# Batched attention and a gated FFN on one core: exponentials between FFN groups, two chunk orders, and a first batch loaded in four-row pieces

## The chip, the cores and the metric

One NeuronCore of a Trainium2 chip runs the whole kernel as one program. The metric is the time of an execution on the device in microseconds (us). Engines: PE (matmuls), DVE, ACT and POOL (elementwise work), SP (it only issues DMAs here); each takes its instructions in program order. ACT and POOL have queues of their own from which they can issue DMAs as well.

## The reference

Attention for 8 batches of 8 heads, 576 queries of 64 elements, with 16 "beacon" keys that every query sees and a causal mask on the other 576 keys; then a gated FFN over all 4608 tokens. Everything comes in and goes out as float32.

```python
k_all = concatenate([beacon_k, k], axis=2)          # 16 + 576 keys
v_all = concatenate([beacon_v, v], axis=2)
scores = scale * q @ k_all.T                        # per batch and head
scores = where(causal, -1e9, scores)                # causal only over the 576
a = exp(scores - scores.max(-1)); a /= a.sum(-1) + 1e-9
x = (a @ v_all), heads side by side                 # 4608 x 512
out = (maximum(x @ w_gate, 0) * (x @ w_val)) @ w_out  # 512 -> 1536 -> 512
```

## The kernel before, in words

Attention works on a pair of heads at a time: four pairs `p` per batch, head `a` of the pair on partitions 64a to 64a+63. Keys lie on partitions in the scores, so no maximum is taken: exponentials are computed directly, and the sum over keys comes from a second matmul against ones. Queries are cut into three chunks (CHUNKS): 240, 256 and 80 columns. The scores of a pair are made in four steps (STEPS): step 0 holds the whole first chunk (368 columns a head), steps 1 and 2 the middle chunk (512 and 384 columns), step 3 the last chunk against all five key tiles (400 columns). So a batch has 16 steps.

- `qk` (L257) issues a step's score matmuls into a PSUM tile `s` (two buffers). `softmax` (L267) is one exponential on ACT over both heads (L270) into `e` (four buffers) and one or two masks by affine_select on POOL (L273).
- `av` (L279) multiplies `e` with `v` and with ones into `o` (two buffers). After the last step of a chunk DVE takes the reciprocal of the sums (L300), multiplies (L302) and writes `xT`, the FFN's input; SP stores the reciprocals in `rsum` (L304) for a check at the end. `r` has three buffers.
- `Ffn.up` (L313) is one group: four gate matmuls (L320), a ReLU on ACT (L323), four up matmuls (L326), and DVE's product into `hT` (L328). Gate and up both take a buffer of the PSUM pool `f`, which has two. `Ffn.down` (L330) is a group of 12 matmuls (L333) for 128 tokens, copied by ACT (L336) and stored by SP. A tile of 512 tokens has 12 up groups and 4 down groups; the first tile is cut at token 240.
- `Batch` holds `qT`, `kT` and `v` of a batch (two buffers of each). A unit is q, k or v in a tile of 128 rows; 15 units per batch. `load` (L214, DMA at L220) fetches 128 rows of all 8 heads, 256 bytes a row and head, into `raw` (eight buffers); k and v have the 16 beacon rows in front. `cast` (L231, L238) turns it to bf16 (batch 0: k on DVE, q on ACT, v on POOL; later batches: POOL). `turn` (L240, L243) is a DMA transpose of q or k, issued by SP.
- The weights come by POOL's DMA queue (L248), cast on the way, gate and value matrix in four parts each, the output matrix `wo` whole.

The order is written out by hand (`manual_schedule`). L370 to L379 load six units of batch 0, cast and turn them, ask for the first two weight parts, and load the rest. `later` holds actions for a step: casts, turns, weights, and the `fetch` of the next batch (from step 16b+1, for batch 1 from step 3: loads at 3/4 of a step each, the cast two steps on, the turn three). The main loop (L418) goes in strides of two steps: for each of them its actions, `qk` and `softmax`; then two FFN groups from `queue`; then `av` of the two steps of the stride before. `ready` (L410) tells after which step how many tokens are through, and with that a tile's groups enter the queue. What is left of the queue runs after the loop, with a count over `rsum` after its fourth group.

Of the kernel before, what the change touches and what calls it, by code (L numbers as in the profile page):

```python
# [10 lines left out]
FP32 = mybir.dt.float32  # L11
BF16 = mybir.dt.bfloat16
# [20 lines left out]
CHUNKS = ((0, 240, 0, 0), (240, 256, 1, 2), (496, 80, 3, 3))  # L33
# [113 lines left out]
def kernel(  # L147
# [12 lines left out]
    nc = tc.nc  # L160
    B, H, S, D = q.shape
    Nb = beacon_k.shape[2]
    P = 128
    d_model = H * D
# [3 lines left out]
    NP = H // 2  # L168
    NKT = 5
    Stot = Nb + S  # L170
# [6 lines left out]
    ident = const.tile([P, P], BF16, name="ident")  # L177
# [10 lines left out]
    main = ctx.enter_context(ExitStack())  # L188
    kvq = main.enter_context(tc.tile_pool(name="kvq", bufs=2))
    stage = main.enter_context(tc.tile_pool(name="stage", bufs=8))  # L190
    half = main.enter_context(tc.tile_pool(name="half", bufs=6))
# [6 lines left out]
    f_ps = main.enter_context(tc.tile_pool(name="f_ps", bufs=2, space=bass.MemoryType.PSUM))  # L198
# [46 lines left out]
    UNITS = [(x, t) for t in range(NKT) for x in "kqv"]  # L245
# [11 lines left out]
    def qk(pr, i):  # L257
        s = s_ps.tile([P, 2, 512], FP32, name="s")
        for (kt, q0, n, c, _, _) in STEPS[i]:
            for a in range(2):  # L260
                rows = slice(a * D, (a + 1) * D)
                nc.tensor.matmul(s[:, a, c:c + n],  # L262
                                 pr.batch.kT[rows, pr.p, kt * P:(kt + 1) * P],
                                 pr.batch.qT[rows, pr.p, q0:q0 + n], start=True, stop=True)
        pr.s[i] = s

    def softmax(pr, i):  # L267
        n = STEP_COLS[i]
        e = psb.tile([P, 2, 512], BF16, name="e")
        nc.scalar.activation(e[:, :, :n], pr.s[i][:, :, :n], AF.Exp, scale=scale)  # L270
        for (kt, q0, _, c, m, base) in STEPS[i]:
            if m:
                nc.gpsimd.affine_select(  # L273
                    out=e[:, :, c:c + m], in_=e[:, :, c:c + m],
                    pattern=[[0, 2], [1, m]], compare_op=ALU.is_ge, fill=0.0,
                    base=base, channel_multiplier=-1)
        pr.e[i] = e

    def av(pr, i):  # L279
        ci = CHUNK_OF_STEP[i]  # L280
        cq0, cn, first, last = CHUNKS[ci]
        if i == first:
            pr.o[ci] = o_ps.tile([P, 2, 256], FP32, name="o")
        o = pr.o[ci]
        e = pr.e[i]
        for j, (kt, q0, n, c, _, _) in enumerate(STEPS[i]):
            kr = min(P, Stot - kt * P)
            for part in range(2):
                for a in range(2):
                    rows = slice(a * D, (a + 1) * D)  # L290
                    c0 = (2 * pr.p + a) * D
                    w = pr.batch.v[:kr, kt, c0:c0 + D] if part == 0 else ones[:kr, :]
                    nc.tensor.matmul(  # L293
                        o[rows, part, q0 - cq0:q0 - cq0 + n], w, e[:kr, a, c:c + n],
                        start=(i == first and j == 0 and part == 0),
                        stop=(i == last and j == len(STEPS[i]) - 1),
                        skip_group_check=True)
        if i == last:
            r = nrm.tile([P, 256], FP32, name="r")
            nc.vector.reciprocal(r[:, :cn], o[:, 1, :cn])  # L300
            t0 = pr.batch.b * S + cq0
            nc.vector.tensor_mul(xT[:, pr.p, t0:t0 + cn], o[:, 0, :cn], r[:, :cn])  # L302
            g = 2 * (pr.batch.b * NP + pr.p)
            nc.sync.dma_start(rsum[g:g + 2, cq0:cq0 + cn],  # L304
                              r.rearrange("(a x) n -> a x n", a=2)[:, 0, :cn])
# [38 lines left out]
    def count_in_range():  # L344

        rows = 2 * B * NP
        ge = const.tile([rows, S], FP32, name="ge")
        nc.vector.tensor_scalar(out=ge, in0=rsum, scalar1=1e-10, scalar2=None, op0=ALU.is_ge)
        nc.vector.scalar_tensor_tensor(out=ge, in0=rsum, scalar=1e10, in1=ge,
                                       op0=ALU.is_le, op1=ALU.mult)  # L350
        ok = const.tile([rows, 1], BF16, name="ok")
        nc.vector.tensor_reduce(ok, ge, op=ALU.min, axis=AX.X)
        cnt_ps = o_ps.tile([1, 1], FP32, name="o")
        nc.tensor.matmul(cnt_ps, ok, ones[:rows, :1], start=True, stop=True)
        cnt = const.tile([1, 1], mybir.dt.int32, name="cnt")
        nc.vector.tensor_copy(cnt, cnt_ps)
        return nc.values_load(cnt, min_val=0, max_val=rows,
                              skip_runtime_bounds_check_because="a count of rows")
# [6 lines left out]
    weights.append(lambda: load_w(wo, moe_w_out, 0, d_model))  # L365

    with tc.manual_schedule():
        batches = [Batch(0)]
        copies = {"k": nc.vector.tensor_copy, "q": nc.scalar.copy, "v": nc.gpsimd.tensor_copy}
        for u in UNITS[:6]:  # L370
            batches[0].load(*u)
        for u in UNITS[:6]:
            batches[0].cast(*u, copies[u[0]])
            if u[0] != "v":
                batches[0].turn(*u)
        for w in weights[:2]:
            w()
        for u in UNITS[6:]:
            batches[0].load(*u)  # L379


        later = {}

        def at(step, action):
            later.setdefault(step, []).append(action)

        for j, u in enumerate(UNITS[6:]):
            at(j // 3, lambda u=u: batches[0].cast(*u, copies[u[0]]))
            if u[0] != "v":
                at(j // 3, lambda u=u: batches[0].turn(*u))  # L390
        for j, w in enumerate(weights[2:]):
            at(j, w)

        def fetch(b, s0):
            at(s0, lambda: batches.append(Batch(b)))
            for j, u in enumerate(UNITS):
                s = s0 + j * 3 // 4
                at(s, lambda u=u: batches[b].load(*u))
                at(s + 2, lambda u=u: batches[b].cast(*u, nc.gpsimd.tensor_copy))
                if u[0] != "v":  # L400
                    at(s + 3, lambda u=u: batches[b].turn(*u))

        work, ready = [], {}
        for b in range(B):
            for c, (_, _, first, last) in enumerate(CHUNKS):
                for p in range(NP):
                    for i in range(first, last + 1):
                        work.append((b, p, i))
                done = (b * S + CHUNKS[c][0] + CHUNKS[c][1])
                ready[len(work)] = done  # L410
            if b + 1 < B:
                fetch(b + 1, 16 * b + (1 if b else 3))


        spans = [(0, 240), (240, 512)] + [(m, m + M_TILE) for m in range(M_TILE, n_tokens, M_TILE)]
        queue, have, pairs = [], 0, {}
        STRIDE = 2
        for s0 in range(0, len(work) + STRIDE, STRIDE):  # L418
            have = ready.get(s0 - STRIDE, have)
            while spans and spans[0][1] <= have:  # L420
                t0, t1 = spans.pop(0)
                f = ffn_tiles[t0 // M_TILE]
                c0, c1 = t0 - f.m0, t1 - f.m0
                queue += f.groups(c0, c1, c0 // P, c1 // P)
            for s in range(s0, s0 + STRIDE):
                for act in later.pop(s, []):
                    act()
                if s < len(work):
                    b, p, i = work[s]
                    pr = pairs.setdefault((b, p), Pair(batches[b], p))  # L430
                    qk(pr, i)
                    softmax(pr, i)
            for g in queue[:STRIDE]:
                g()
            del queue[:STRIDE]
            for s in range(s0 - STRIDE, s0):
                if 0 <= s < len(work):
                    b, p, i = work[s]
                    av(pairs[b, p], i)
        for t0, _ in spans:  # L440
            queue += ffn_tiles[t0 // M_TILE].groups(0, M_TILE, 0, M_TILE // P)
        for j, g in enumerate(queue):
            if j == 4:
                in_range = count_in_range()
            g()
# [33 lines left out]
```

## Time and profile before

| | us |
|---|---|
| Median of 2 runs | 486.41 (485.93 to 486.9) |
| Profiled execution | 484.15 |
| Its span, first to last instruction | 482.4 |
| PE busy | 394.4 (82%) |
| DVE busy | 239.8 (50%) |
| ACT busy | 190.3 (39%) |
| POOL busy | 132.0 (27%) |
| Mean granted clock of the PE, of full speed | 0.975 |

A profile has a page (busy time, 40 slices of the span, DMA queues, the chain of work that ended last) and views of the trace: timelines of an engine, windows with the busy time of each engine, waits. An idle time in brackets names what ended it. A line that begins with a time is an instruction or several alike: start and length in us, engine, line of the kernel, operation, out<-in. Several matmuls overlap in their pipeline, so the end of a group lies some 0.16 us after the PE can begin the next.

### The profile page before, as it was taken

The page shows a single profiled execution, that of the slowest core. Times are in us where ns is not written, and L with a number is a line of the kernel's source. Part 1 is how long each engine was busy: PE and PEld are TensorE (multiplying, and loading weights), DVE is VectorE, ACT ScalarE, POOL GpSimd, SP SyncE. Part 2 cuts the span into 40 slices and gives each one's busy share as a digit, 9 for nine tenths or more (in the row PEclk, how much of TensorE's full clock was granted, in tenths as well). Part 3 has the DMA queues.
Part 4 walks back from the last instruction along what each step waited for, and adds up shares of the span by engine and source line. Part 5 has one row for each costly group of instructions (what it writes and reads, how often), then busy time and mean ns, then how long its engine had stood idle before and what let it go on. Part 6 is the DMA issues. An engine that isn't in the chain of part 4 may idle for free.

```text
span 482.4 us, 9099 instructions
## 1 busy us (share of the span) xinstructions
PE 394.4 (82%) x3505; PEld 204.2 (42%) x3505; DVE 239.8 (50%) x322; ACT 190.3 (39%) x290; POOL 132.0 (27%) x293
## 2 busy tenths in 40 slices
PE   0113848777989998999899989998998899799994
PEld 0012635454434544454454445544454454244442
DVE  0033525855486448636762777277528653330320
ACT  2122414444445344534443445354444442122321
POOL 2162135343424332423251335134421110000000
PEclk9998859999999999999999999999999999899998
DMA  9999997695569257824793396439720001002002
GB/s 163 191 198 194 134 198 118 136 202 105 135 108 180 72 133 139 170 72 111 164 145 108 86 175 130 118 81 192 102 89 3 1 18 73 0 1 87 1 13 80
DMA packets 166145, 53.37 MB, mean 111 GB/s; under 512 B 155728, under 2 KB 161488, under 8 KB 166096
## 3 DMA queue, kind: packets, MB, share of 16 engines
q1 hardware_dynamic: 160320, 48.01, 49.2%
q0 software_dynamic: 5776, 4.72, 7.0%
q8 instruction: 29, 0.48, 0.4%
q14 instruction: 20, 0.16, 0.1%
HBM read 38.27 MB, written 9.44 MB: 99 GB/s over the span
## 4 chain that ended last, share of the span: by engine, by line
PE 52%; DMA 13%; SPq 9%; issue 8%; ACT 8%; DVE 5%; POOL 3%; ACTq 0%; DVEq 0%; POOLq 0%
PE f L333 19%; PE f L320 11%; PE f L326 11%; PE o L293 7%; DMA raw<-in_v_dram 6%; ACT g L323 5%; SPq L220 5%; DMA raw<-in_k_dram 5%; SPq L243 4%; DVE r L300 4%; PE s L262 3%; ACT e L270 3%; DMA raw<-in_q_dram 2%; POOL e L273 1%; POOL v L238 1%
## 5 line engine op out<-in xcount | busy, mean ns | idle before, releaser
L300 DVE RECIPROCAL r<-o 128x240 f32<-128x240 f32 (+2 forms) x96 | 129.9, 1353 | 91.4 <-PE o L293 76.3
L270 ACT ACTIVATE e<-s 128x736 bf16<-128x736 f32 (+3 forms) x128 | 103.7, 861 | 104.9 <-PE s L262 103.6
L320 PE MATMUL f<-xT,wg 128*128 128x512 bf16 (+2 forms) x480 | 116.2, 364 | 25.8 <-ACT g L323 16.4
L328 DVE TENSOR_TENSOR hT<-g,f 128x512 bf16<-128x512 f32 (+2 forms) x120 | 75.9, 633 | 106.5 <-PE f L326 92.4
L326 PE MATMUL f<-xT,wv 128*128 128x512 bf16 (+2 forms) x480 | 115.4, 364 | 9.3 <-ACT g L323 9.2
L323 ACT ACTIVATE g<-f 128x512 f32<-128x512 f32 (+2 forms) x120 | 66.8, 557 | 89.8 <-PE f L320 89.8
L333 PE MATMUL f<-wo,hT 128*128 128x512 bf16 x432 | 96.2, 379 | 0.7 <-ACT g L323 0.7
L273 POOL TENSOR_SCALAR_AFFINE_SELECT e<-e 128x256 bf16<-128x256 bf16 (+2 forms) x160 | 58.8, 388 | 96.8 <-ACT e L270 96.5
L326 PEld LDWEIGHTS <-wv 128*128 128x128 bf16 x480 | 47.6, 99 | 70.1 <-issue 26.9
L320 PEld LDWEIGHTS <-wg 128*128 128x128 bf16 x480 | 43.4, 99 | 72.0 <-issue 38.0
L238 POOL CAST half<-raw 128x512 bf16<-128x512 f32 (+1 forms) x70 | 42.4, 613 | 103.8 <-DMA raw<-in_q_dram 71.6
L293 PE MATMUL o<-e,v 128*64 128x80 bf16 (+3 forms) x704 | 57.8, 238 | 9.9 <-POOL e L273 9.8
L262 PE MATMUL s<-qT,kT 64*128 64x80 bf16 (+2 forms) x704 | 36.1, 236 | 33.3 <-DMA qT<-half 25.2
L333 PEld LDWEIGHTS <-hT 128*128 128x128 bf16 x432 | 41.1, 98 | 49.9 <-issue 2.0
L293 PE MATMUL o<-e,ones 128*64 128x80 bf16 (+3 forms) x704 | 53.9, 233 | 0.0
L293 PEld LDWEIGHTS <-v 128*64 128x64 bf16 (+1 forms) x704 | 35.6, 111 | 36.1 <-issue 35.2
L336 ACT COPY ob<-f 128x512 f32<-128x512 f32 x36 | 21.1, 586 | 67.4 <-PE f L333 67.4
L238 POOL CAST v<-raw 128x512 bf16<-128x512 f32 (+1 forms) x40 | 24.5, 613 | 61.9 <-DMA raw<-in_v_dram 61.9
L262 PEld LDWEIGHTS <-kT 64*128 64x128 bf16 x704 | 21.6, 98 | 40.1 <-issue 25.8
L302 DVE TENSOR_TENSOR xT<-o,r 128x240 bf16<-128x240 f32 (+2 forms) x96 | 34.3, 357 | 3.3
L293 PEld LDWEIGHTS <-ones 128*64 128x64 bf16 (+1 forms) x704 | 34.9, 112 | 0.1
L238 DVE CAST half<-raw 128x512 bf16<-128x512 f32 (+1 forms) x5 | 2.4, 477 | 24.5 <-DMA raw<-in_k_dram 24.5
(19 smaller groups left out, 17.0 us busy)
## 6 DMA issues: line engine op xcount, KB each, us to landing
out_dram<-ob SPq DMA_DIRECT2D x36, 256.0 KB
raw<-in_q_dram SPq DMA_DIRECT2D x32, 256.0 KB
raw<-in_k_dram SPq DMA_DIRECT2D x24, 256.0 KB
raw<-in_v_dram SPq DMA_DIRECT2D x24, 256.0 KB
raw<-in_k_dram SPq DMA_DIRECT2D x8, 224.0 KB
raw<-in_v_dram SPq DMA_DIRECT2D x8, 224.0 KB
wg<-in_moe_w_gate_dram POOLq DMA_DIRECT2D x4, 384.0 KB, 6.2
wv<-in_moe_w_val_dram POOLq DMA_DIRECT2D x4, 384.0 KB, 7.3
```

Of the source, the lines that this page charges most:

```text
L238: copy(dst, self.raw[x, t][:n])
L262: nc.tensor.matmul(s[:, a, c:c + n], pr.batch.kT[rows, pr.p, kt * P:(kt + 1) * P], pr.batch.qT[rows, pr.p, q0:q0 + n], start=True, stop=True)
L270: nc.scalar.activation(e[:, :, :n], pr.s[i][:, :, :n], AF.Exp, scale=scale)
L273: nc.gpsimd.affine_select(out=e[:, :, c:c + m], in_=e[:, :, c:c + m], pattern=[[0, 2], [1, m]], compare_op=ALU.is_ge, fill=0.0, base=base, ...
L293: nc.tensor.matmul(o[rows, part, q0 - cq0:q0 - cq0 + n], w, e[:kr, a, c:c + n], start=(i == first and j == 0 and part == 0), stop=(i == la ...
L300: nc.vector.reciprocal(r[:, :cn], o[:, 1, :cn])
L302: nc.vector.tensor_mul(xT[:, pr.p, t0:t0 + cn], o[:, 0, :cn], r[:, :cn])
L320: nc.tensor.matmul(g[:, :n], wg[:, ki, nf * P:(nf + 1) * P], x[:, ki], start=(ki == 0), stop=(ki == KM - 1))
L323: nc.scalar.activation(gs[:, :n], g[:, :n], AF.Relu)
L326: nc.tensor.matmul(u[:, :n], wv[:, ki, nf * P:(nf + 1) * P], x[:, ki], start=(ki == 0), stop=(ki == KM - 1))
L328: nc.vector.tensor_mul(self.h[:, nf, c0:c1], gs[:, :n], u[:, :n])
L333: nc.tensor.matmul(o, self.h[:, nf, ms * P:(ms + 1) * P], wo[:, nf, :], start=(nf == 0), stop=(nf == NF - 1))
```

## The change

Three things change in the order that the kernel writes out; what is computed stays.

1. In the loop, all actions and both `qk` of a stride come first; then the first `softmax`, one FFN group, the second `softmax`, the other group.
2. From batch 1 on, a batch's steps run as steps 1 and 2 of all four pairs, then steps 0 and 3 of all four pairs. Its tokens count as ready only when the whole batch is through. Batch 0 keeps its order.
3. Batch 0's q and k: rows 0 to 511 of a pair of heads are loaded with four rows to a partition (1 KB in one piece), SP's queue for k and ACT's for q; a cast regroups them, four PE transposes into an `f` tile turn them, and a copy spreads the columns (`turn_pair`). The last 64 rows, with the beacons for k, are a tile of all heads (`turn_tail`). v is loaded as before. The DMA transposes of batch 0 go. The weights' later parts are asked for two per step.

```diff
     with tc.manual_schedule():
-        batches = [Batch(0)]
-        copies = {"k": nc.vector.tensor_copy, "q": nc.scalar.copy, "v": nc.gpsimd.tensor_copy}
-        for u in UNITS[:6]:
-            batches[0].load(*u)
-        for u in UNITS[:6]:
-            batches[0].cast(*u, copies[u[0]])
-            if u[0] != "v":
-                batches[0].turn(*u)
+        b0 = Batch(0)
+        batches = [b0]
+        WIDE = 4 * P
+        rest = S - WIDE
+        start = main.enter_context(tc.tile_pool(name="start", bufs=1))
+        tails = {}
+        wide = {}
+
+        def load_pair(x, src, p, eng):
+            t = wide[x, p] = start.tile([P, 2, 4 * D], FP32, name=f"wide_{x}{p}")
+            eng.dma_start(t, src[0, 2 * p:2 * p + 2, :WIDE].rearrange("h (p r) d -> p h (r d)", r=4))
+
+        def load_tail(x, src, beacon, eng):
+            t = tails[x] = start.tile([P, d_model], FP32, name=f"tail_{x}")
+            for p0, a in ((0, src[0, :, WIDE:]), (rest, beacon)):
+                if a is not None:
+                    eng.dma_start(t[p0:p0 + a.shape[1]].rearrange("p (h d) -> p h d", d=D),
+                                  a.rearrange("h p d -> p h d"))
+
+        def turn_pair(x, p, copy):
+            h = half.tile([P, 4, P], BF16, name="half")
+            copy(h.rearrange("x r (h d) -> x h r d", d=D),
+                 wide[x, p].rearrange("x h (r d) -> x h r d", d=D))
+            ps = f_ps.tile([P, 4, P], BF16, name="f")
+            for r in range(4):
+                nc.tensor.transpose(ps[:, r], h[:, r], ident)
+            dst, off = (b0.kT, Nb) if x == "k" else (b0.qT, 0)
+            copy(dst[:, p, off:off + WIDE].rearrange("x (p r) -> x p r", r=4),
+                 ps.rearrange("x r p -> x p r"))
+
+        def turn_tail(x, copy):
+            n = rest + (Nb if x == "k" else 0)
+            h = half.tile([P, d_model], BF16, name="half")
+            copy(h[:n], tails[x][:n])
+            ps = f_ps.tile([P, NP, P], BF16, name="f")
+            for p in range(NP):
+                nc.tensor.transpose(ps[:, p, :n], h[:n, p * P:(p + 1) * P], ident[:n, :n])
+            if x == "k":
+                copy(b0.kT[:, :, Nb + WIDE:Stot], ps[:, :, :rest])
+                copy(b0.kT[:, :, :Nb], ps[:, :, rest:n])
+            else:
+                copy(b0.qT[:, :, WIDE:], ps[:, :, :rest])
+
+        load_pair("k", k, 0, nc.sync)
+        load_pair("q", q, 0, nc.scalar)
+        load_tail("k", k, beacon_k[0], nc.sync)
+        load_pair("q", q, 1, nc.scalar)
+        load_pair("k", k, 1, nc.sync)
+        for p in (2, 3):
+            load_pair("q", q, p, nc.scalar)
+        load_tail("q", q, None, nc.scalar)
+        for t in range(2):
+            b0.load("v", t)
+        for p in (2, 3):
+            load_pair("k", k, p, nc.sync)
+        for t in range(2, NKT):
+            b0.load("v", t)
+        turn_pair("k", 0, nc.vector.tensor_copy)
+        turn_pair("q", 0, nc.scalar.copy)
+        turn_tail("k", nc.vector.tensor_copy)
+        turn_pair("k", 1, nc.vector.tensor_copy)
+        turn_pair("q", 1, nc.scalar.copy)
+        b0.cast("v", 0, nc.gpsimd.tensor_copy)
+        b0.cast("v", 1, nc.gpsimd.tensor_copy)
         for w in weights[:2]:
             w()
-        for u in UNITS[6:]:
-            batches[0].load(*u)
...
-        for j, u in enumerate(UNITS[6:]):
-            at(j // 3, lambda u=u: batches[0].cast(*u, copies[u[0]]))
-            if u[0] != "v":
-                at(j // 3, lambda u=u: batches[0].turn(*u))
+        for p in (2, 3):
+            at(p - 1, lambda p=p: turn_pair("k", p, nc.vector.tensor_copy))
+            at(p - 1, lambda p=p: turn_pair("q", p, nc.scalar.copy))
+        at(3, lambda: turn_tail("q", nc.vector.tensor_copy))
+        for t in range(2, NKT):
+            at(t - 1, lambda t=t: b0.cast("v", t, nc.gpsimd.tensor_copy))
         for j, w in enumerate(weights[2:]):
-            at(j, w)
+            at(j // 2, w)
...
         for b in range(B):
-            for c, (_, _, first, last) in enumerate(CHUNKS):
-                for p in range(NP):
-                    for i in range(first, last + 1):
-                        work.append((b, p, i))
-                done = (b * S + CHUNKS[c][0] + CHUNKS[c][1])
-                ready[len(work)] = done
+            if b == 0:
+                for c, (c0, cn, first, last) in enumerate(CHUNKS):
+                    work += [(b, p, i) for p in range(NP) for i in range(first, last + 1)]
+                    ready[len(work)] = b * S + c0 + cn
+            else:
+                work += [(b, p, i) for p in range(NP) for i in (1, 2)]
+                work += [(b, p, i) for p in range(NP) for i in (0, 3)]
+                ready[len(work)] = (b + 1) * S
...
-            for s in range(s0, s0 + STRIDE):
+            now = [s for s in range(s0, s0 + STRIDE) if s < len(work)]
+            for s in now:
                 for act in later.pop(s, []):
                     act()
-                if s < len(work):
-                    b, p, i = work[s]
-                    pr = pairs.setdefault((b, p), Pair(batches[b], p))
-                    qk(pr, i)
-                    softmax(pr, i)
-            for g in queue[:STRIDE]:
-                g()
-            del queue[:STRIDE]
+                b, p, i = work[s]
+                qk(pairs.setdefault((b, p), Pair(batches[b], p)), i)
+            for j in range(STRIDE):
+                if j < len(now):
+                    b, p, i = work[now[j]]
+                    softmax(pairs[b, p], i)
+                if queue:
+                    queue.pop(0)()
```

## Rows read from the trace of the kernel before

**Rows 1.** The page: PE and DMA busy in 40 slices, tenths

```profile
PE   0113848777989998999899989998998899799994
...
DMA  9999997695569257824793396439720001002002
```

**Rows 2.** The chain of waits: start, length; down groups that open a batch's steps

```profile
119.76 5.29 PE f L333 x24
...
399.45 5.29 PE f L333 x24
```

**Rows 3.** Windows, sum over nine stretches of batch 5, 259.81 to 306.50

```profile
sum 46.69, PE 43.69 PEld 22.05 DVE 28.18 ACT 21.82 POOL 16.28; mean PE 4.85 PEld 2.45 DVE 3.13 ACT 2.42 POOL 1.81
```

**Rows 4.** Timeline of PE in batch 5

```profile
273.67 1.02 PE L320 MATMUL f<-xT,wg 128*128 128x512 bf16 x4 [0.39 <-ACT g L323]
275.37 1.02 PE L326 MATMUL f<-xT,wv 128*128 128x512 bf16 x4 [0.69 <-ACT g L323]
...
283.40 0.56 PE L262 MATMUL s<-qT,kT 64*128 64x256 bf16 x8
283.88 1.04 PE L320 MATMUL f<-xT,wg 128*128 128x512 bf16 x4
284.76 1.03 PE L326 MATMUL f<-xT,wv 128*128 128x512 bf16 x4
286.10 1.02 PE L320 MATMUL f<-xT,wg 128*128 128x512 bf16 x4 [0.31 <-ACT g L323]
```

**Rows 5.** Timeline of ACT, the stride from 283.40

```profile
283.83 1.73 ACT L270 ACTIVATE e<-s 128x1024 bf16<-128x1024 f32 x2 [2.33 <-PE s L262]
285.44 0.60 ACT L323 ACTIVATE g<-f 128x512 f32<-128x512 f32 x1
```

**Rows 6.** Timeline of DVE in batch 5

```profile
259.07 0.66 DVE L300 RECIPROCAL r<-o 128x80 f32<-128x80 f32 x1 [4.01 <-PE o L293]
...
259.92 0.65 DVE L300 RECIPROCAL r<-o 128x80 f32<-128x80 f32 x1
...
270.91 1.65 DVE L300 RECIPROCAL r<-o 128x240 f32<-128x240 f32 x1
...
272.92 1.65 DVE L300 RECIPROCAL r<-o 128x240 f32<-128x240 f32 x1
...
283.51 1.76 DVE L300 RECIPROCAL r<-o 128x256 f32<-128x256 f32 x1
285.30 0.42 DVE L302 TENSOR_TENSOR xT<-o,r 128x256 bf16<-128x256 f32 x1
286.08 0.69 DVE L328 TENSOR_TENSOR hT<-g,f 128x512 bf16<-128x512 f32 x1 [0.36 <-ACT g L323]
```

**Rows 7.** Timeline of the start, batch 0 to batch 1's first scores

```profile
11.38 1.22 SPq L243 DMA_TRANSPOSE qT<-half  x1
...
16.96 0.80 PE L262 MATMUL s<-qT,kT 64*128 64x240 bf16 x8 [16.96 <-DMA qT<-half]
...
48.35 0.36 PE L320 MATMUL f<-xT,wg 128*128 128x240 bf16 x1 [6.94 <-DVE xT L302]
...
78.09 0.49 PE L262 MATMUL s<-qT,kT 64*128 64x240 bf16 x8
```

**Rows 8.** DMA queues: packets, MB, share of 16 engines' span (q0 carries the weights)

```profile
q1 hardware_dynamic: 160320, 48.01, 49.2%
q0 software_dynamic: 5776, 4.72, 7.0%
```

**Rows 9.** Timeline of SP's queue: loads of batch 1, a turn in batch 5

```profile
58.78 3.77 SPq L220 DMA_DIRECT2D raw<-in_k_dram  x1
...
78.09 0.58 SPq L220 DMA_DIRECT2D raw<-in_v_dram  x1
...
294.53 1.24 SPq L243 DMA_TRANSPOSE qT<-half  x1
```

**Rows 10.** Timeline of POOL: a cast of batch 1

```profile
63.92 0.61 POOL L238 CAST half<-raw 128x512 bf16<-128x512 f32 x1 [13.45 <-DMA raw<-in_q_dram]
```

## The prediction, made before the result was known

> **What bounds the kernel now.** I read the page's slices first, then the chain of waits, then one batch closely, then the start. The slices [rows 1] show three stretches: about eight slices (100 us) in which the PE fills slowly while the DMA engines are full, a long plateau at 9 to 10 tenths, and a PE-bound end. In the chain [rows 2] the down matmuls that open a batch's steps return every 46.6 us from batch 2 (119.8) to the end of batch 7 (399.5): six equal periods, so one period decides 280 us. The windows over the period from 259.81 add up to 46.69 us with the PE busy 43.69 [rows 3]: 3.0 us per batch in which the PE stands still. What it waits for stands behind its rows in the timeline: the gate and the up matmuls wait for ACT's ReLU [rows 4].
>
> The timelines of PE, ACT and DVE show how. In a stride the PE does two scores steps, then gate 0, up 0, gate 1, up 1, then the output steps of the stride before. There are only two `f` buffers, so gate 1 needs ReLU 0 done. ACT has both exponentials ahead of ReLU 0: at 283.83 they start, together 1.73 us, and ReLU 0 begins at 285.44 [rows 5]; gate 1 starts at 286.10 although up 0, begun at 284.76, frees the PE some 0.87 later, at 285.63 [rows 4]. The shown idle (0.31) counts from the modelled end of the last matmul; the time lost is 0.47. Where DVE still works off two 240-column chunks (two reciprocals of 1.65 and their products [rows 6]), up 1 waits as well: 0.39 + 0.69 shown, about 1.4 lost with 0.16 on each. A batch has two such strides (2.8), two of the 0.47 kind (0.94), and about 0.3 in each of the two others (0.6): 4.3 us per batch, and 42.4 us would be left without any wait.
>
> The start: the first scores are at 16.96, the first finished FFN gate at 48.35, and batch 1's scores at 78.09 [rows 7]. From there batch 1's steps last some 41 us, to just before 119.76 [rows 2], and there the PE is not the limit: loading, casting and turning the next batch is.
>
> **Part 1: ACT's order.** PE's order stays. ACT now has exp 0, ReLU 0, exp 1, ReLU 1. Let T be the start of a stride's scores (283.40). Gate 0 starts at T+0.49, its last result is out at T+1.53; exp 0 started at T+0.43 and takes about 0.92 of the 1.73, so ReLU 0 runs T+1.57 to 2.17, and the PE, free at T+2.23, finds gate 1's buffer ready. Those waits go. ReLU 1 now stands behind exp 1, at T+3.3 to 3.9; its readers, the product 1 and a later stride, come later than that. What is late next is DVE's product 0, which frees the buffer for up 1 (PE ready at T+3.09). After a stride with a middle chunk, DVE does one reciprocal of 1.76 and a product of 0.42 and is free by T+2.32; up 0's result comes at T+2.5, so product 0 (0.69) ends at T+3.19: 0.14 lost with the signalling.
>
> **Part 2: chunks in turn.** From batch 1 on, four strides do the middle chunk, then four do the 240- and the 80-column chunk. DVE's debt per stride is then 2.2 (middle) or 2.01 + 0.85 = 2.86 (240 and 80, from the starts of successive reciprocals [rows 6]), instead of 4.0, 2.2 and 1.7. With 2.86, product 0 ends at T+3.53 and up 1 loses 0.48. Of the six strides with gate and up groups, four follow a middle chunk (4 x 0.14), one a 240/80 pair (0.48). The other one, the second of a batch, has a new wait: an FFN tile is now released only when its whole batch is through, with no group left over in the queue, and its first gate needs the 240 columns of the last pair, whose output step ended just before. That reciprocal and product are ready at about T+1.85; the gate's fourth matmul wants them at T+1.14: 0.71, and 0.14 later in the stride. Sum: 0.56 + 0.48 + 0.85 = 1.9 per batch against 4.3, so 2.4 saved; six periods give 14. Ends: all waits gone, 6 x 4.3 = 26; or up 1 waits for ReLU 1 (first rival), minus 7. The queue of groups doesn't run dry: two per stride, 16 per tile, eight strides per batch. After the last stride tile 7 meets the same late chunk without scores in front: +1.
>
> The earlier casts of the second step (all actions now come ahead of both softmaxes) can hold POOL's masks back. The masked tiles are read a stride later, 5 us on, and that covers it; the cost without this cover is the cast's wait, 1 to 5 us once.
>
> **Part 3: the first batch.** Ten DMA transposes go (SP's queue loses 10 x 1.2 us of issuing [rows 7], and the waits for casts that stand in front of them), and q and k come in four-row pieces. The queue rows [rows 8] give 0.492 x 482.4 x 16 / 160320 = 23.7 ns for a packet of the load queue (300 B on average) and 93.5 ns for one of the weights' (817 B written). The 256-byte rows of all loads are some 113,000 of those packets, the outputs 4,600; the remaining 42,000 belong to 80 transposes, 0.78 us of all engines each. Batch 0 cost 14,080 packets (20.9 us) + 7.8. Afterwards: v 4,736 and the tails 1,152 packets (8.7 us), and 2,048 packets of 1 KB, whose price the trace doesn't show: between 23.7 and 93.5 ns, 3 to 12 us; I take 7, near the middle: a piece of 1 KB is larger than either average, but the weights' packets are read at twice their size and cast. So 15.7 instead of 28.7: 13 us of DMA work less (8 to 17). "DMA: Bandwidth & Descriptors" of the Trainium skill (Specifications) says that transfers of 512 B or more run at line rate, about 27 GiB/s per engine; by that the 1 KB pieces would take 35 ns, 4.5 us in all, and the start would gain 2.5 more. No run here shows it.
>
> Forty PE transposes and some twenty copies come in. Eight scores matmuls took 0.80 at 16.96, so 0.1 each: 4 us of a PE that otherwise waits; the copies on DVE and ACT are of the size of an `hT` product or a ReLU, 0.6 to 0.7, beside the loads. "TensorE: Matmul & The Clock Gate" (Part 4: PE-mode transpose) of the Trainium skill speaks against this part: about 275 ns for one in a kernel, 11 us in all; 20 stand ahead of the first scores, which would then come 3.5 later. No transpose on the PE is in this trace.
>
> The first scores come near 10 instead of 17, the first gate near 30 to 38 instead of 48 (pair 2's load stands on PE, ACT and DVE ahead of the second scores; v tile 2's cast ahead of weights and masks on POOL). How much of that lasts to batch 1 is set by DMA: the weights (0.07 x 482.4 = 34 us of all engines) still have to come, now asked for by step 3 instead of 6, and take the share of the loads behind them. Once they are in, batch 1's units follow at the pace of SP's chain of turn, load, cast: 19.3 us for the eight from 58.78 to 78.09 [rows 9], 2.4 each. If the weights end about 11 us sooner (13 of work at a DMA share near 1.2), but one or two units fewer are in by then, 8 us remain. Bounds 0 and 16. Batch 1's own 41 us stay, being set by the same chain.
>
> **Sum.** 484.15 (the profiled execution, span 482.4) - 8 - 14 + 1 = 463. The median of the runs is 486.4, 2.3 above it; I forecast 465 for the measurement. It can tell about 2%, 9.7 us, from no change.
>
> **Rivals.** A: the wait moves to up 1. Which of the two `f` buffers up 1 gets is fixed when the program is built; at 275.37 it waited for ReLU 1 [rows 4], elsewhere for the product. ReLU 1 now ends at T+3.9: 0.86 lost instead of 0.14 in five strides, +3.6 per batch, and part 1 and 2 together cost 1.2 per batch: 465 + 22 = 487. For it: the built order did choose ReLU 1 once; against: there it was the earlier of the two, here it is later by 0.4 to 0.7. B: the start gives nothing, because weights in front of batch 0's last tiles hold POOL: 473. For it: a cast of batch 1 on POOL waited 13.5 us behind `wo` [rows 10]; against: the bytes do go. C: the start keeps all its lead (16): 457. D, the other side: the first step of a batch is now a middle chunk and needs k and q tiles 0 to 3 turned, not two of each. The turn of the fourth q tile is issued at 294.53 [rows 9], over at 295.8; a turn issued till 12.6 was used at 16.96 [rows 7], 4.4 later; so it lands near 300.2, and the next batch starts at 306.0, half a microsecond before its down group at 306.50 (the end of the window of [rows 3]): 5.8 us to spare, 3.4 when batches are 2.4 shorter. If loading slips beyond that, each us costs 7 (seven boundaries); from 3 us on the kernel is no faster than before, and at 5 us it takes 500.
>
> **How the numbers follow.** Forecast 0.55 (459 to 471), B 0.20, C 0.15, A 0.07, D 0.03. B's slow end (0.03) and A are within 2%; D alone is slower. Faster 0.87, same 0.10, slower 0.03. 453 to 477 holds the forecast, most of B and C.
>
> **What would show it.** Right: a period of about 44.3 between down groups; no wait of gate 1 for ReLU 0; up 1 waiting for DVE by 0.1 to 0.5; the fourth matmul of a tile's first gate waiting for `xT`, 0.7, once per batch; batch 1's scores near 70; scores of a batch never waiting for `qT`. Wrong: a period of 46 or more, up 1 behind ReLU 1, waits for `qT<-half` at batch starts, or batch 1 not before 78.

## The result, and the profile after

The changed kernel takes 459.59 us (2 runs, 457.66 to 461.52) against 486.41; the ratio is 0.9448, with a 95% interval of 0.9273 to 0.9624. Run again beside its own variants (last table) it gave 0.9438 (0.9388 to 0.9489). It is faster, by about 5.5%.

| | before | after |
|---|---|---|
| Profiled execution, its span | 484.15, 482.4 | 461.52, 459.8 |
| PE busy, share of the span | 394.4 (82%) | 405.0 (88%) |
| First scores | 16.96 | 11.66 |
| First FFN gate done by | 48.7 | 32.5 |
| Second q load of batch 1 cast (POOL) | 63.92 | 50.37 |
| First scores of batch 1 | 78.09 | 67.05 |
| Down groups at the start of batch 2 | 119.76 | 108.63 |
| Down groups at the end of batch 7 | 399.45 | 374.51 |

The last two rows are the chain's; with the span's end they split the gain: 11.1 us of lead at batch 2, 13.8 more over the six periods behind it, and 2.3 given back after the loop. Together 22.6, the difference of the spans. The profiled run of the changed kernel is the slower of its two and the one before is below its median, so between the medians the gain is larger, 26.8.

The slices of the page after, beside [rows 1]: the PE is at 9 tenths for the first time in the seventh slice, and from the tenth it stays there until the loop is over; the DMA engines are still full at the start, but for five slices in a row instead of six.

```profile
PE   2547569869999999999999999999999997899994
...
DMA  9999965893495449545944793568310010002002
```

The chain of waits after, with the down groups that answer to [rows 2], and one period between them (286.21 to 330.61):

```profile
108.63 5.29 PE f L333 x24
...
286.21 5.29 PE f L333 x24
...
330.61 5.29 PE f L333 x24
...
374.51 5.29 PE f L333 x24
```

The period is 44.3 (265.88 / 6; 44.40 in the batch shown) instead of 46.6. The PE's timeline after, in that batch: the second stride of the batch (from 292.23), one after a middle chunk (from 298.06) and the one after a 240/80 pair (from 318.21).

```profile
292.23 0.56 PE L262 MATMUL s<-qT,kT 64*128 64x256 bf16 x8
292.72 0.82 PE L320 MATMUL f<-xT,wg 128*128 128x512 bf16 x3
294.13 0.38 PE L320 MATMUL f<-xT,wg 128*128 128x512 bf16 x1 [0.59 <-DVE xT L302]
...
298.06 0.56 PE L262 MATMUL s<-qT,kT 64*128 64x256 bf16 x8
298.55 1.04 PE L320 MATMUL f<-xT,wg 128*128 128x512 bf16 x4
299.43 1.03 PE L326 MATMUL f<-xT,wv 128*128 128x512 bf16 x4
300.29 1.03 PE L320 MATMUL f<-xT,wg 128*128 128x512 bf16 x4
301.30 1.02 PE L326 MATMUL f<-xT,wv 128*128 128x512 bf16 x4
...
318.21 0.51 PE L262 MATMUL s<-qT,kT 64*128 64x240 bf16 x14
...
320.39 1.03 PE L320 MATMUL f<-xT,wg 128*128 128x512 bf16 x4
321.77 1.02 PE L326 MATMUL f<-xT,wv 128*128 128x512 bf16 x4 [0.35 <-DVE hT L328]
```

Gate 1 (300.29) follows up 0 (299.43) after 0.86, the PE's own pace; in [rows 4] it came 1.34 after. Up 1 (301.30) comes 1.01 after gate 1, so it loses 0.15, and 1.38 after it at 321.77, which loses 0.5. The fourth matmul of the tile's first gate, 294.13, waits for `xT`. ACT's and DVE's timelines after show why:

```profile
298.56 1.02 ACT L270 ACTIVATE e<-s 128x1024 bf16<-128x1024 f32 x1 [1.69 <-PE s L262]
299.63 0.60 ACT L323 ACTIVATE g<-f 128x512 f32<-128x512 f32 x1
300.12 0.81 ACT L270 ACTIVATE e<-s 128x768 bf16<-128x768 f32 x1
301.35 0.60 ACT L323 ACTIVATE g<-f 128x512 f32<-128x512 f32 x1 [0.43 <-PE f L320]
```

```profile
291.98 1.66 DVE L300 RECIPROCAL r<-o 128x240 f32<-128x240 f32 x1 [3.63 <-PE o L293]
293.67 0.41 DVE L302 TENSOR_TENSOR xT<-o,r 128x240 bf16<-128x240 f32 x1
...
298.17 1.76 DVE L300 RECIPROCAL r<-o 128x256 f32<-128x256 f32 x1
299.97 0.42 DVE L302 TENSOR_TENSOR xT<-o,r 128x256 bf16<-128x256 f32 x1
300.56 0.69 DVE L328 TENSOR_TENSOR hT<-g,f 128x512 bf16<-128x512 f32 x1 [0.17 <-PE f L326]
```

ReLU 0 starts 1.07 after exp 0 instead of 1.61 [rows 5], and exp 1 follows it. The product 0 (300.56 to 301.25) is what up 1 waits for at 301.30. The `xT` of the last 240-column chunk is written by 294.08, and the gate goes on at 294.13. The list of waits for 100 to 370 us has only this for the PE (us in total, times, the longest):

```profile
PE f L320 <- DVE xT L302: 3.6, 6, 0.6
PE f L326 <- DVE hT L328: 2.1, 6, 0.4
PE f L326 <- ACT g L323: 0.5, 1, 0.5
```

The start after, on PE and POOL, against [rows 7] and [rows 10]:

```profile
10.70 1.03 PE L394 MATMUL f<-ident,half 128*128 128x128 bf16 x8 [1.98 <-DVE half L390]
11.66 0.49 PE L262 MATMUL s<-qT,kT 64*128 64x240 bf16 x4
...
32.13 0.36 PE L320 MATMUL f<-xT,wg 128*128 128x240 bf16 x1 [4.72 <-DVE xT L302]
...
67.05 0.56 PE L262 MATMUL s<-qT,kT 64*128 64x256 bf16 x8 [2.58 <-DMA rsum<-r]
```

```profile
50.37 0.61 POOL L238 CAST half<-raw 128x512 bf16<-128x512 f32 x1 [7.00 <-DMA raw<-in_q_dram]
...
67.35 0.61 POOL L238 CAST v<-raw 80x512 bf16<-80x512 f32 x1 [1.21 <-DMA raw<-in_v_dram]
```

The casts of batch 1 come 13.5 us sooner from the second q load on, and the rest of the batch takes as long as before: 16.98 from this cast to the last one of v, against 16.96 (63.92 to 80.88). Ahead of it `wo`, the last of the weights, is asked for at 22.34 and takes 27.0 us to land (last figure of its row in the list of DMA issues):

```profile
wo<-in_moe_w_out_dram POOLq DMA_DIRECT2D x1, 1536.0 KB, 27.0
```

### The profile page after: what moved, and what is told of

It reads as the page before. It is cut to its first block, busy times and chain, and to the rows that moved or that the text cites. A ratio compares the mean times of both kernels' runs of the same rounds, so it can differ in the third digit from the quotient of the medians.

```text
span 459.8 us, 9167 instructions
## 1 busy us (share of the span) xinstructions
PE 405.0 (88%) x3545; PEld 212.4 (46%) x3545; DVE 243.9 (53%) x330; ACT 196.0 (43%) x293; POOL 132.0 (29%) x293
## 4 chain that ended last, share of the span: by engine, by line
PE 68%; DMA 13%; DVE 8%; SPq 3%; issue 3%; ACT 2%; POOL 1%; ACTq 0%; DVEq 0%; POOLq 0%
PE f L333 21%; PE f L326 18%; PE f L320 16%; PE o L293 8%; DMA raw<-in_v_dram 6%; DVE r L300 5%; PE s L262 4%; DMA raw<-in_k_dram 2%; SPq L243 2%; DMA raw<-in_q_dram 1%; ACT e L270 1%; DMA wide_k_131<-in_k_dram 1%; SPq L220 1%; DMA wide_q_120<-in_q_dram 1%; DVE hT L328 1%
## 5 line engine op out<-in xcount | busy, mean ns | idle before, releaser
L270 ACT ACTIVATE e<-s 128x736 bf16<-128x736 f32 (+3 forms) x128 | 110.1, 863 | 108.7 <-PE s L262 106.8
L320 PE MATMUL f<-xT,wg 128*128 128x512 bf16 (+2 forms) x480 | 120.7, 374 | 11.1 <-DVE xT L302 9.4
L326 PE MATMUL f<-xT,wv 128*128 128x512 bf16 (+2 forms) x480 | 117.0, 368 | 6.2 <-ACT g L323 3.3
L273 POOL TENSOR_SCALAR_AFFINE_SELECT e<-e 128x256 bf16<-128x256 bf16 (+2 forms) x160 | 57.3, 387 | 88.6 <-ACT e L270 88.6
L293 PE MATMUL o<-e,v 128*64 128x80 bf16 (+4 forms) x704 | 58.8, 241 | 13.6 <-POOL e L273 13.6
L320 PEld LDWEIGHTS <-wg 128*128 128x128 bf16 x480 | 44.8, 102 | 48.5 <-issue 8.8
L293 PEld LDWEIGHTS <-v 128*64 128x64 bf16 (+1 forms) x704 | 37.5, 113 | 39.6 <-issue 37.4
L293 PE MATMUL o<-e,ones 128*64 128x80 bf16 (+4 forms) x704 | 53.7, 236 | 0.0
L262 PE MATMUL s<-qT,kT 64*128 64x80 bf16 (+3 forms) x704 | 37.1, 239 | 2.6 <-DMA rsum<-r 2.6
L394 PE MATMUL f<-ident,half 128*128 128x128 bf16 x32 | 4.5, 309 | 10.2 <-DVE half L390 9.2
```

The lines of the kernel that those rows point to most:

```text
L262: nc.tensor.matmul(s[:, a, c:c + n], pr.batch.kT[rows, pr.p, kt * P:(kt + 1) * P], pr.batch.qT[rows, pr.p, q0:q0 + n], start=True, stop=True)
L273: nc.gpsimd.affine_select(out=e[:, :, c:c + m], in_=e[:, :, c:c + m], pattern=[[0, 2], [1, m]], compare_op=ALU.is_ge, fill=0.0, base=base, ...
L293: nc.tensor.matmul(o[rows, part, q0 - cq0:q0 - cq0 + n], w, e[:kr, a, c:c + n], start=(i == first and j == 0 and part == 0), stop=(i == la ...
L320: nc.tensor.matmul(g[:, :n], wg[:, ki, nf * P:(nf + 1) * P], x[:, ki], start=(ki == 0), stop=(ki == KM - 1))
L326: nc.tensor.matmul(u[:, :n], wv[:, ki, nf * P:(nf + 1) * P], x[:, ki], start=(ki == 0), stop=(ki == KM - 1))
```

## The experiments

### The three parts, each alone

Part 1 alone:

```diff
-            for s in range(s0, s0 + STRIDE):
+            now = [s for s in range(s0, s0 + STRIDE) if s < len(work)]
+            for s in now:
...
-                    qk(pr, i)
-                    softmax(pr, i)
-            for g in queue[:STRIDE]:
-                g()
-            del queue[:STRIDE]
+                b, p, i = work[s]
+                qk(pairs.setdefault((b, p), Pair(batches[b], p)), i)
+            for j in range(STRIDE):
+                if j < len(now):
+                    b, p, i = work[now[j]]
+                    softmax(pairs[b, p], i)
+                if queue:
+                    queue.pop(0)()
```

> Part 1 alone: the kernel before with one softmax, one FFN group, the other softmax, the other group; chunk order and start as before. Theory (the waits of gate 1 and up 1 behind ACT are what part 1 takes away, and up 1 then falls back on the earlier of ReLU 1 and DVE's product): gate 1 waits nowhere, the two strides after two 240-column chunks still lose 0.86 each, two after a middle chunk 0.14: 2.0 instead of 4.3 per batch, period 44.4, time about 472. Rival (the turn of long and short chunks is what frees DVE, and the order on ACT alone only moves the wait to up 1): period 46 or more, time 482 to 486.

Part 2 alone, the kernel before with

```diff
-            for c, (_, _, first, last) in enumerate(CHUNKS):
...
+            else:
+                work += [(b, p, i) for p in range(NP) for i in (1, 2)]
+                work += [(b, p, i) for p in range(NP) for i in (0, 3)]
+                ready[len(work)] = (b + 1) * S
```

> Part 2 alone: the kernel before with steps 1 and 2 of all pairs, then 0 and 3 of all pairs from batch 1 on; both exponentials still ahead of both ReLUs. Theory: gate 1 still waits 0.3 to 0.47 in five strides, the tile's first gate waits 0.7 for xT; up 1 loses its long wait: 2.8 lost per batch, period 45.2, time about 477. Rival (the chunk order carries the gain): period 44.4, time 472.

Part 3 alone, the kernel before with the changed kernel's lines up to `def fetch`:

```diff
-        batches = [Batch(0)]
...
+        b0 = Batch(0)
+        batches = [b0]
...
-            at(j, w)
+            at(j // 2, w)
```

> Part 3 alone: the kernel before with the new load and turn of batch 0 and the weights two parts per step; loop as before. Theory: the lead of 11 us at the first down groups of batch 2 comes from here alone and stays to the end, the period stays 46.69: time about 475. Rival (the start's lead depends on the new loop order too, since the loop's ACT order frees the stalled strides of batches 0 and 1): lead 5 or less, time 481 or more.

Parts 1 and 2 together, the two diffs above with the old start:

> Parts 1 and 2 without part 3: the old start. Theory: period 44.4 as in the changed kernel, which is no better than part 1 alone, because what the chunk order gives (0.7 less at up 1 in two strides) it takes back with the wait for xT and the longer DVE debt: time about 472, within 2 of part 1 alone. Rival (chunks in turn and ACT order need each other): 5 or more below part 1 alone.

Measured, beside the kernel before on the same chip (485.06):

| | us | ratio (95%) | expected |
|---|---|---|---|
| Part 1 alone | 472.85 | 0.9744 (0.9713 to 0.9774) | 472 |
| Part 2 alone | 477.47 | 0.9846 (0.9826 to 0.9867) | 477 |
| Part 3 alone | 471.27 | 0.9725 (0.9705 to 0.9746) | 475 |
| Parts 1 and 2 | 472.04 | 0.9737 (0.9716 to 0.9758) | 472 |

The start and the loop add up: 13.8 from part 3 and 13.0 from parts 1 and 2 make 26.8, and the whole change gives 0.0562 of 486, 27. Inside the loop they don't: the order on ACT is worth 12.2 by itself, the chunks in turn 7.6 by themselves, and nothing that can be measured on top of the order on ACT. The PE's timelines show the periods, first with part 1 alone, then with part 2 alone:

```profile
300.09 5.35 PE L333 MATMUL f<-wo,hT 128*128 128x512 bf16 x24
...
344.77 5.35 PE L333 MATMUL f<-wo,hT 128*128 128x512 bf16 x24
...
358.01 1.03 PE L320 MATMUL f<-xT,wg 128*128 128x512 bf16 x4
359.72 1.02 PE L326 MATMUL f<-xT,wv 128*128 128x512 bf16 x4 [0.69 <-ACT g L323]
```

```profile
301.16 5.35 PE L333 MATMUL f<-wo,hT 128*128 128x512 bf16 x24
...
346.46 5.35 PE L333 MATMUL f<-wo,hT 128*128 128x512 bf16 x24
```

44.68 and 45.30, where 44.4 and 45.2 had been expected. With part 1 alone gate 1 waits nowhere, and two strides per batch keep the wait of up 1, 0.69 shown, 0.86 lost, as at 359.72; the list of waits of this run puts all twelve of them down to ACT's ReLU, at 359.72 to ReLU 1 (359.07 to 359.67). With both parts that wait goes and the wait for `xT` comes, and the period is 44.4 (252.36 to 296.76 in the run of parts 1 and 2). The rivals of all four runs are out. Part 3 did better than its expectation (below).

### What the new order of chunks pays for

The last two strides of a batch, in the changed kernel:

```diff
-                work += [(b, p, i) for p in range(NP) for i in (0, 3)]
+                work += [(b, p, i) for p in (0, 1) for i in (0, 3)]
+                work += [(b, p, i) for i in (0, 3) for p in (2, 3)]
```

> The changed kernel, but the last two strides of a batch take step 0 of pairs 2 and 3, then step 3 of pairs 2 and 3. Theory (0.85 per batch and 1.1 after the loop are the wait for xT of the last 240-column chunk and the DVE debt behind it): the chunk is done a stride earlier, its two heavy reciprocals fall beside down groups, only stride 6 (0.48) and four strides of 0.14 remain; period 43.5 instead of 44.4, no wait of gate 1 for xT, time 6 below the changed kernel, about 453. Rival (the two 240-column chunks side by side cost at up 1 or hold SP's loads up what they give): period 44.3 or more, time as the changed kernel.

Measured: 453.69, ratio 0.9332 (0.9277 to 0.9388), where the changed kernel has 0.9438. The period (PE's timeline of this run) is 43.67:

```profile
283.73 5.35 PE L333 MATMUL f<-wo,hT 128*128 128x512 bf16 x23
...
290.58 0.81 PE L320 MATMUL f<-xT,wg 128*128 128x512 bf16 x3 [0.16 <-issue]
291.22 1.03 PE L326 MATMUL f<-xT,wv 128*128 128x512 bf16 x4
...
327.40 4.92 PE L333 MATMUL f<-wo,hT 128*128 128x512 bf16 x21
```

(The trace lacks a matmul in some groups.) The first gate of the tile, 290.58, passes straight into up 0: no wait for `xT` is left in its list of waits. 0.73 per batch instead of 0.85, and 453.69 where 453 was expected; the rival is out.

### What carries the start

The wide loads in rows of 256 bytes. With them each head has a DMA of its own and the copy back is contiguous; the cast, the PE transposes and the queues are kept:

```diff
-            eng.dma_start(t, src[0, 2 * p:2 * p + 2, :WIDE].rearrange("h (p r) d -> p h (r d)", r=4))
+            for a in range(2):
+                eng.dma_start(t[:, a].rearrange("p (r d) -> p r d", r=4),
+                              src[0, 2 * p + a, :WIDE].rearrange("(r p) d -> p r d", r=4))
...
-            copy(dst[:, p, off:off + WIDE].rearrange("x (p r) -> x p r", r=4),
-                 ps.rearrange("x r p -> x p r"))
+            copy(dst[:, p, off:off + WIDE], ps.rearrange("x r p -> x (r p)"))
```

> The changed kernel, but the wide loads of batch 0 fetch row r*128+p into partition p (256 bytes a piece, one DMA per head); cast, PE transposes and copies stay, the copy back is contiguous. Theory (most of the start's lead is the dropped DMA transposes and SP's waits for them; the 1 KB pieces save some 35 of 95 ns per four rows, 4.5 us of DMA work): first scores 1 to 2 later, lead at batch 2 smaller by 3, time 3 above the changed kernel, about 462. Rival 1 (the four-row pieces carry the start): 8 or more above. Rival 2 (DMA is not what the start waits for): within 1.

The weights one per step:

```diff
-            at(j // 2, w)
+            at(j, w)
```

> The changed kernel with the weights' later parts asked for one per step instead of two. Theory (the DMA engines are full until the weights and batch 1 are in, whatever the order): time within 2 of the changed kernel. Rival (weights asked for early push batch 0's and 1's loads back and hold POOL): 3 or more faster, with batch 1's scores earlier than 67; the opposite (weights late at the FFN's groups): gate matmuls wait for a weight and it is 2 or more slower.

Batch 1 in the old order:

```diff
-            if b == 0:
+            if b <= 1:
```

> The changed kernel with batch 1, too, in the old chunk order; from batch 2 on as changed. Theory (the new order makes batch 1's first scores wait for the turn of the fourth q and k tiles, 2.6 us at 67.05, and this is why part 3 alone led by 13.4 at batch 2's down groups and the changed kernel only by 11.1): batch 1 starts without that wait, the lead becomes 13, time 2 below the changed kernel, about 457.5. Rival (the wait is made up for by the loading chain that follows): within 1 of the changed kernel.

| changed kernel with | us | ratio (95%) | its first down groups of batch 2 at |
|---|---|---|---|
| rows of 256 bytes | 464.45 | 0.9553 (0.9491 to 0.9615) | 111.90 |
| weights one per step | 458.92 | 0.9436 (0.9377 to 0.9496) | 106.19 |
| batch 1 in the old order | 457.94 | 0.9449 (0.9387 to 0.9510) | 106.26 |

The short rows cost some 5.6 us (0.0115 of 486, from 0.9438), between the theory's 3 and the first rival's 8; the intervals of the two ratios allow either. ACT's DMA queue, which carries only q here, gives the price of a piece. Of the changed kernel, then of the short rows:

```profile
q10 hardware_dynamic: 1616, 1.18, 1.0%
```

```profile
q10 hardware_dynamic: 4752, 1.18, 1.6%
```

0.016 x 463.5 x 16 / 4752 is 25.0 ns for a packet of the short rows. The changed kernel's queue has 1,024 pieces of 1 KB and 592 others, 73.6 us in all; with 25.0 for each of the others a piece of 1 KB takes 57. These shares are rounded, and the others need not cost the same. The single packets in the two traces give 62 ns for a piece of 1 KB and 26 for one of 256 bytes, on the mean: 62 where four rows cost 104. For q and k together, if k's cost the same, that is 7.9 us of all engines against 13.3, and the difference, 5.4, is about what the short rows cost in time. "DMA: Bandwidth & Descriptors" of the Trainium skill (Specifications) has line rate from 512 bytes on; at its 27 GiB/s per engine a piece of 1 KB would take 35 ns, an estimate. These runs have 62, with other queues active on the same engines, and the measurement decides.

The weights' pace makes no difference, as expected. In this run `wo` was asked for ten us later, at 32.40, and landed sooner after it:

```profile
wo<-in_moe_w_out_dram POOLq DMA_DIRECT2D x1, 1536.0 KB, 17.1
```

So it was in at 49.5, against 49.3 in the changed kernel, and the second q load of batch 1 was cast at 50.69, against 50.37. Within these ten us, when it is asked for does not decide when it is in. The short rows, which add work to the full DMA engines, do put it off: it was asked for at 24.38 and in 27.4 later, at 51.8, and that cast is at 53.33.

Batch 1's order makes no difference either, and there my theory falls: the wait of 2.58 at 67.05 goes (that run's scores of batch 1 start at 64.27 without one), but nothing is left of it in the time. The profile puts the wait of 2.58 down to `rsum<-r`, stored by the same engine SP. That it is one for a turn is read from the last turn of `qT` that these scores need, issued at 63.06; in the two other runs of this table the same wait (2.81 and 1.58) is put down to `qT<-half`.

What the rest of part 3's gain owes to the dropped DMA transposes, to ACT's queue and to the turn on the PE was not taken apart.

### After the loop

The changed kernel again; the changed kernel with the count cut in parts (DVE's part stays after the fourth group, the PE's sum comes four groups later, the value is read at the end); this with the late pairs, the order of the last two strides tried above; and these with batch 1 in the old order:

```diff
             if j == 4:
-                in_range = count_in_range()
+                ok = count_rows()
+            if j == 8:
+                cnt = count_sum(ok)
             g()
+        in_range = count_load(cnt)
```

> The changed kernel itself, as the reference for the three beside it. Both theories: as in its first measurement, a ratio of 0.945 to the kernel before, near 459.

> The changed kernel with the count over rsum cut in two: DVE's part after the fourth group behind the loop as before, the PE's matmul four groups later, the value loaded at the end. Theory (after the loop the PE stands some 3.5 us for DVE's count, and the granted clock falls to half behind that, for 6.8 us in the changed kernel against 3.4 before; this, beside 1.1 for the late chunk, is why the tail grew by 2.3): the PE doesn't stop, the clock stays at full there, 3.5 + 3.4 = 5 to 7 less, about 453. Rival (the clock falls at that place anyway, or DVE's work is only put off to the end): 3 or less.

> The late count and the order of the last two strides (step 0 of pairs 2 and 3, then step 3 of both) together. Theory: their gains lie in different places and add up: 6 + 6, about 447. Rival (the late chunk after the loop and the count are one wait): 450 or more.

> The run before this one with batch 1 in the old chunk order as well. Theory (batch 1's wait for its turned tiles, 2.6 us, is gained in the lead at batch 2's down groups, 106.3 instead of 108.6, and stays to the end): 2 less than without it, about 445. Rival (it is lost again in batch 1's own strides): within 1.

| | us | ratio (95%) |
|---|---|---|
| changed kernel | 459.51 | 0.9438 (0.9388 to 0.9489) |
| late count | 454.21 | 0.9346 (0.9304 to 0.9389) |
| late count, late pairs | 448.76 | 0.9235 (0.9196 to 0.9273) |
| these and batch 1 in the old order | 448.66 | 0.9236 (0.9194 to 0.9278) |

The two gains add up, 5.3 and 5.4 (4.5 and 5.4 by the ratios; the late pairs without the late count had given 5.2); batch 1's order again gives nothing. The PE's timelines of the changed kernel (first profile) and of the late count, at the count:

```profile
392.06 0.16 PE L354 MATMUL o<-ones,ok 64*1 64x1 bf16 x1 [2.78 <-DVE ok L352]
392.96 1.86 PE L320 MATMUL f<-xT,wg 128*128 128x512 bf16 x4 [0.74 <-DVE cnt L356]
```

```profile
390.01 1.02 PE L326 MATMUL f<-xT,wv 128*128 128x512 bf16 x4 [0.69 <-ACT g L323]
...
394.70 0.16 PE L357 MATMUL o<-ones,ok 64*1 64x1 bf16 x1
394.80 1.04 PE L320 MATMUL f<-xT,wg 128*128 128x512 bf16 x4
```

In the changed kernel the PE stands 2.78 + 0.74 for DVE, and the group behind takes 1.86 instead of 1.04. The windows (length, then busy time of each engine, granted clock before the DMA share) show the clock, of the changed kernel and of the late count:

```profile
391.00:396.00 5.00, 3.20 (x9) 1.26 (x10) 1.11 (x3) 0.60 (x1) 0.00 (x0) 0.58 0.01 2
396.00:399.00 3.00, 3.00 (x10) 1.04 (x9) 0.69 (x1) 0.60 (x1) 0.00 (x0) 0.56 0.00 0
```

```profile
391.00:396.00 5.00, 5.00 (x24) 2.04 (x22) 2.12 (x4) 1.32 (x3) 0.00 (x0) 1.00 0.00 0
396.00:399.00 3.00, 3.00 (x15) 1.27 (x13) 1.01 (x2) 1.07 (x2) 0.00 (x0) 1.00 0.01 3
```

0.58 and 0.56 mean the lower level, 1.2 GHz, for most of the stretch; without the stop it stays at 2.4. One wait of 0.69 is left, at 390.01. The profile puts it down to a ReLU (over at 389.96); DVE's product ahead of it, held up by the count (387.30 to 389.31), is over only at 389.91; that the count costs this wait is likely, but no run shows it.

## Why the prediction was right, and where it was off

The forecast was 465, the result 459.59: faster, inside 453 to 477 and within the forecast's own 459 to 471, at its lower end. The loop came out as worked out; the start was worth more than taken. Term by term:

- **Part 1** held. Gate 1 waits nowhere, ReLU 0 ends before the PE is free, and product 0 is what is late next: 0.14 were worked out for up 1 after a middle chunk, the trace has 0.15.
- **Part 2** held, down to its drawback. Worked out: 0.71 at the tile's first gate and 0.48 at up 1 of stride six. The trace has 0.59 and 0.35 shown; with the 0.16 between the modelled end and a free PE that is 0.75 and 0.51. The period was forecast at 44.3 and is 44.3. What the prediction did not say, because it summed parts 1 and 2 together, is that part 2 adds nothing to part 1: e5's reordering shows that it could.
- **Part 3** is the term that was mis-sized: 8 taken, 13.8 measured with part 3 alone. The step that failed was "If the weights end about 11 us sooner (13 of work at a DMA share near 1.2), but one or two units fewer are in by then, 8 us remain." `wo` was asked for at 22.3 instead of 47.5 and landed after 27.0 us instead of 15.2: the weights were in at 49.3 instead of 62.7, 13 sooner. Asking at 22.3 was not what it took: asked for at 32.4, in the run with the weights one per step, it was in at 49.5 as well. That less DMA work brought it in sooner fits the run with short rows, but the 13 were not taken apart. And no unit fewer was in: in both kernels four units of batch 1 had been cast when `wo` landed (the last at 42.04 and at 49.14), and the fifth, the second q load, was cast next, at 50.37 and 63.92. The chain behind took its 17 us in both, as the prediction had said. With no discount the term would have been about 13, and the total near 460. How much of this lead is left at batch 2's down groups varies, 10.6 to 14.0 in the eight profiles with this start; the first one's 11.1 is at the low side. The price of a 1 KB piece, taken near the middle of its bounds (7 us for 2,048), measured 62 ns, 7.9 us. For the PE transposes the row behind the estimate (0.1 each) nearly held: eight took 1.03 at 10.70, 0.13 each. The 275 ns for one in "TensorE: Matmul & The Clock Gate" of the Trainium skill (Part 4) are near the 309 ns that one lasts here on the mean. But the eight follow each other faster than that, so these times don't add up. The first scores came at 11.66, not 10; nothing hung on it.
- **After the loop** 1 was taken, 2.3 came: 1.08 shown at the late chunk of tile 7, and the rest is the longer stretch at 1.2 GHz behind the count: the two up groups behind it take 6.24 (392.96 to 399.20) where the kernel before has 5.14 (416.70 to 421.84).

The rivals: A (up 1 behind ReLU 1) did not come in the changed kernel, but for one wait of 0.5 between 100 and 370 us. Its mechanism and its 0.86 did come with part 1 alone, in two strides per batch, and the chunks in turn took it away; the prediction had not said that A hangs on part 2. B (nothing from the start) is out by part 3 alone. C (the start keeps all its lead, 457) came nearest in the size of its term, and in the time: 2.6 away, the forecast 5.4. D's mechanism showed once, at batch 1's first scores, where the loads are late (2.6, if that wait is one for a turn as read above); at later batches the scores wait for no turn, and the run without that wait was no faster.

## What to carry to other kernels

Where two PSUM buffers go round between the PE and a reader, as here, look at the order on the reader: put the reader's short evacuation ahead of long work that nobody waits for, and then look for the second reader (here DVE's product), for it is the next limit. A producer that finishes just before its consumer's first use should get one stage of distance; here two swapped strides were worth 5 us. A serial check on a small value belongs where the PE need not stop for it: here the stop cost the clock behind it as well.

## What was not expected

- The same start code put batch 2's first down groups at 108.6 and 107.1 in two profiles of the changed kernel, and at 105.8 with the late count, which touches nothing before the loop's end. What makes the difference is not known. I had read 108.6 against 106.3 (part 3 alone) as a cost of the new order; it lies within this spread, and the two runs with batch 1 in the old order (106.3 and 109.1) say the same.
- The stretch at the lower clock behind the count was not equally long for the same kernel. In the second profile of the changed kernel the slow groups are over sooner than in the first, where the group at 396.33 still took 1.91:

```profile
393.13 1.51 PE L326 MATMUL f<-xT,wv 128*128 128x512 bf16 x4
394.48 1.03 PE L320 MATMUL f<-xT,wg 128*128 128x512 bf16 x4
```

- Asked for ten us later, `wo` landed at the same time. What would bring it in sooner, beside less work for the DMA engines, was not tried.
